# Attention on one core: V's gate logits carried beside V, tokens on partitions, and another split of PSUM

## The chip, the cores and the metric

One core of one Trainium2 chip. The time is device microseconds of one execution. The kernel before took 1797.77 us at the median of three runs (1797.65 to 1798.2).

## What is computed

An attention whose keys and values are averages over eight neighbours feeds a top-2 mixture of eight experts, and that feeds a dense block. Cut to what matters:

```python
# q, k, v: 8 batches, 8 heads, 576 tokens, head dimension 64
k_p, v_p = mean of k, v over groups of 8 tokens          # 72 per head
attn = softmax(q @ k_p.T / 8)                            # 576 x 72
x = (attn @ v_p), heads side by side                     # 4608 tokens x 512

logits = x @ w_gate                                      # 8 experts
noisy = logits + log1p(exp(x @ w_noise)) * noise
top 2 of noisy, softmax over the two
out = sum over the two experts of weight * (relu(x @ w1[e]) @ w2[e])

h = out @ w_in;  result = (h - tanh(h)) @ w_out
```

## The kernel before

The program runs three stages after each other: `attention` (L1113 on), `moe` and `Moe2`. The first takes some 252 of 1796 us. Its work is 36 tiles of 128 tokens (`NT`), and a hand-written loop of `NT + 6` steps at its end issues, in each step, one stage of several tiles: exponentials of tile t, the transposes of the weights of tile t - 2 (`st_attT`), q's transposes of tile t + 2 (`st_q`), the scores of tile t + 1, the gate projection of tile t - 5 (`st_x`), the scaling of tile t - 6 (`st_g`), and last the weights times V of tile t - 3 (`st_av`). Every engine takes its instructions in the order in which this loop issues them; tiles in PSUM are handed on as soon as their reader is through.

A batch has 576 tokens, four and a half tiles, so tiles 4, 13, 22 and 31 belong to two batches. The 576 keys of eight heads (72 each) lie on partitions in five chunks of 128, 128, 128, 96 and 96 (`cuts`), so a chunk holds parts of up to three heads. For each batch `prep_jobs` averages k and v by halving adds (on GpSimd first, then VectorE), finds V's largest magnitude (`vmaxT`), makes a power-of-two scale from it and builds `VB`, a block matrix of V in which columns of a head are zero on rows of other heads (`vscale`, masked by `of`), and builds `KB` for the scores (`kbd`). The steps of these jobs are fixed relative to the batch's first tile `T0`; `chain` and `fixed` place VectorE's other work (the weights of the first expert: `amax`, `low`) in the steps with the least planned load.

Weights times V (L1349 to L1359) holds V as the stationary operand and the transposed weights as the moving one, so the result has features on partitions; ScalarE copies it (`st_xT`, L1361), and `st_x` (L1365) multiplies it with `wgn`, an identity with the gate's and the noise's columns beside it, which turns tokens onto partitions and makes 16 logits a head pair at once. `st_g` (L1376) reads both from `px`, divides by the softmax sums, writes x to DRAM and collects the logits.

```python
nc.tensor.matmul(p[:, m, o:o + n], VB[b % 2][:w, c, j:j + 128], a[:w, c, o:o + n], ...)      # st_av
nc.tensor.matmul(p[:, m, 0:128 + 4 * E], xT[:, m], wgn[:, m], start=True, stop=True)         # st_x
tt(xr..., h(p[:, :, 0:128], D), r..., op=OP.mult)                                            # st_g, L1381
tt(lg[:, t - t0], h(p[:, :, 128:128 + 4 * E], 2 * E), r..., op=OP.mult)                      # st_g, L1387
```

PSUM has eight banks: `px` one buffer of two banks, `pt` four buffers (transposes, V products, all batch jobs and gates), `psc` two (one per half of a tile's scores).

Groups of tiles (up to 9, 19, 28 and 35) go through `gate_jobs`, a chain of some 45 small VectorE operations that `tick` spreads over the steps; `tick_pe` lets one TensorE part of it through per step. After the second group `early_x` gathers the first expert's first 512 tokens. The last steps (t from 36) have no scores any more and a few idle matmuls (`warm`).

In `moe`, units of L1 and L2 follow each other with a lag of two; after the first group's last unit (`u == KF - 1`) two L2 are issued, then the transposes `tr` of the second group's three blocks through PSUM (L333 to L336), then the next L1.

Of the kernel before, what the change touches and what calls it, by code (L numbers as in the profile page):

```python
# [186 lines left out]
def moe(nc, tc, st, V, z):  # L187
# [410 lines left out]
    for u in range(len(units) + LAG):  # L598
# [514 lines left out]
def attention(nc, tc, st, V):  # L1113
# [52 lines left out]
    def warm(n, tag="px"):  # L1166

        if tag == "px":
            p = ps.tile([128, HP, 256], F32, name="px", bufs=1)[:, 0:2].rearrange("p a c -> p (a c)")
        else:  # L1170
            p = ps.tile([128, 4 * SP], F32, name=tag, bufs=2)
        for _ in range(n):
            nc.tensor.matmul(p, calm[:, 0:128], calm[:, 0:p.shape[1]], start=True, stop=True)
# [11 lines left out]
    VB = [one.tile([128, 5, 4 * D], F32, name=f"vb{i}") for i in range(2)]  # L1185
# [27 lines left out]
    for i in range(2):  # L1213
        for w, o in ((w_gate, 0), (w_noise, E)):
            o += 128 + 2 * E * i
            nc.sync.dma_start(wgn[64 * i:64 * i + 64, :, o:o + E], w.rearrange("(m i p) e -> i p m e", i=2, p=64)[i])
# [11 lines left out]
    lz = ep.tile([128, NT, 2 * E], F32, name="lz")  # L1228
    def prep_jobs(b, first=False):
# [20 lines left out]
        def vmaxT():  # L1250
            p = ps.tile([1, 128], F32, name="pt", bufs=4)
            nc.tensor.transpose(p, tl["vm"], identf)
            yield
            tl["vx"] = wk.tile([1, 1], F32, name="vx")
            nc.vector.tensor_reduce(tl["vx"], p, axis=AX.X, op=OP.max)

        def vscale():
            p = ps.tile([128, 1], F32, name="pt", bufs=4)
# [4 lines left out]
            of8 = wk.tile([128, 5, 4], F32, name="of8")  # L1263
            ts(of8, of, m[:, 2:3], None, op0=OP.mult)
            (nc.gpsimd if b > 1 else nc.vector).tensor_tensor(VB[b % 2].rearrange("p c (j d) -> p c j d", d=D), tl["va"][:, :, 0:1].to_broadcast([128, 5, 4, D]),
               of8[:, :, :, None].to_broadcast([128, 5, 4, D]), op=OP.mult)
# [7 lines left out]
            ts(isc[:, f0:f1], m[:, 1:2].to_broadcast([128, f1 - f0]), 1.0 / 128, None, op0=OP.mult)  # L1274

        def kbd():
            for i, (c0, c1) in enumerate(((0, 3), (3, 5))):
                w = cuts[c1] - cuts[c1 - 1]
                p = ps.tile([128, 4, 128], F32, name="pt", bufs=4)[:, 0:c1 - c0, 0:w]
# [9 lines left out]
    def st_q(t):  # L1289
        p = ps.tile([128, HP, 128], F32, name="pt", bufs=4)  # L1290
# [20 lines left out]
    def st_exps(t):  # L1311
        at = wk.tile([128, 2, 4, SP], F32, name="at", bufs=3)
        if t in sums:
            SM[0] = wk.tile([128, 5, 2, 4], F32, name="sm"), t
# [5 lines left out]
        if t + 1 in sums or t + 1 == NT:  # L1320
            SM[1] = sm, t0

    def st_norm(t):
        if not (t + 1 in sums or t + 1 == NT):
            tick(2)
            return
        sm, t0 = SM.pop(1)
        sm = sm[:, 0:t + 1 - t0]
        ts(sm, sm, 1e-9, None, op0=OP.add)
        tick()  # L1330
        rc = wk.tile([128, 5, H], F32, name="rc")[:, 0:t + 1 - t0]
# [5 lines left out]
    def st_attT(t):  # L1337
# [3 lines left out]
        for g, (c0, c1) in enumerate(((0, 3), (3, 5))):  # L1341
            w = cuts[c1] - cuts[c1 - 1]
            p = ps.tile([128, 4, 128], F32, name="pt", bufs=4)[:w, 0:c1 - c0]
# [5 lines left out]
    def st_av(t):  # L1349
        a = ATT.pop(t)  # L1350
        p = ps.tile([128, HP, 128], F32, name="pt", bufs=4)
        for o, n, b, s in runs(t):
            for m in range(HP):
                cs = [c for c in range(5) if cuts[c] < 2 * SP * (m + 1) and 2 * SP * m < cuts[c + 1]]
                for c in cs:
                    w, j = cuts[c + 1] - cuts[c], 128 * (m + 1 - c)
                    nc.tensor.matmul(p[:, m, o:o + n], VB[b % 2][:w, c, j:j + 128], a[:w, c, o:o + n],
                                     start=(c == cs[0]), stop=(c == cs[-1]))
        PV[t] = p  # L1359

    def st_xT(t):  # L1361
        XT[t] = wk.tile([128, HP, 128], F32, name="xT")
        nc.scalar.activation(XT[t], PV.pop(t), AF.Copy)

    def st_x(t):  # L1365

        xT = XT.pop(t)
        p = PX[t] = ps.tile([128, HP, 256], F32, name="px", bufs=1)
        for m in range(HP):
            nc.tensor.matmul(p[:, m, 0:128 + 4 * E], xT[:, m], wgn[:, m], start=True, stop=True)  # L1370

    PX = {}
# [3 lines left out]
    def st_g(t):  # L1376
        p, rc = PX.pop(t), RC.pop(t)
        xr = wk.tile([128, DM], F32, name="xr", bufs=3)
        r = rc.rearrange("p (m i) -> p m i", i=2)[:, :, :, None]
        h = lambda a, n: a.rearrange("p m (i n) -> p m i n", n=n)  # L1380
        tt(xr.rearrange("p (m i n) -> p m i n", m=HP, i=2), h(p[:, :, 0:128], D), r.to_broadcast([128, HP, 2, D]), op=OP.mult)  # L1381
        nc.sync.dma_start(x_d[128 * t:128 * t + 128, :], xr)
        if t in sums:
            LG[0] = wk.tile([128, 5, HP, 2, 2 * E], F32, name="lg", bufs=2)
            LG[1] = t
        lg, t0 = LG
        tt(lg[:, t - t0], h(p[:, :, 128:128 + 4 * E], 2 * E), r.to_broadcast([128, HP, 2, 2 * E]), op=OP.mult)  # L1387
# [346 lines left out]
```

## Time and profile before

| | before |
|---|---|
| median of 3 runs | 1797.77 us |
| the profiled execution, its own time | 1798.16 us |
| its span, first to last instruction | 1795.9 us |
| TensorE busy | 1756.3 us (98%) |
| VectorE busy | 1284.9 us (72%) |
| ScalarE busy | 939.9 us (52%) |
| GpSimd busy | 269.8 us (15%) |
| mean granted TensorE clock | 0.995 |

The profile gives for each engine the time in which at least one of its instructions ran. PE is TensorE's matmuls, PEld its weight loads (they overlap matmuls), DVE VectorE, ACT ScalarE, POOL GpSimd, SP the engine that issues most transfers. Matmuls are pipelined: the time between the starts of two is less than the duration shown of one. A matmul of 32-bit numbers appears as two passes, each with its weight load; a transpose as one. An arrow behind an idle time names what ended it.

### The profile page before, as it was taken

The page shows a single profiled execution, that of the slowest core. Times are in us where ns is not written, and L with a number is a line of the kernel's source. Part 1 is how long each engine was busy: PE and PEld are TensorE (multiplying, and loading weights), DVE is VectorE, ACT ScalarE, POOL GpSimd, SP SyncE. Part 2 cuts the span into 40 slices and gives each one's busy share as a digit, 9 for nine tenths or more (in the row PEclk, how much of TensorE's full clock was granted, in tenths as well). Part 3 has the DMA queues.
Part 4 walks back from the last instruction along what each step waited for, and adds up shares of the span by engine and source line. Part 5 has one row for each costly group of instructions (what it writes and reads, how often), then busy time and mean ns, then how long its engine had stood idle before and what let it go on. Part 6 is the DMA issues. An engine that isn't in the chain of part 4 may idle for free. (4 is left out here: it accounts for less than half of the span.)

```text
span 1795.9 us, 28933 instructions
## 1 busy us (share of the span) xinstructions
PE 1756.3 (98%) x10792; PEld 1071.3 (60%) x10792; DVE 1284.9 (72%) x2550; ACT 939.9 (52%) x2249; POOL 269.8 (15%) x264
## 2 busy tenths in 40 slices
PE   7999989999999999999999999999999999999998
PEld 5998864545455454545454454566666666666664
DVE  5688776776767666665665457687887879788775
ACT  5887732434435343434334246575665756566554
POOL 2334101303031030101101102010120201010000
PEclk8999999999999999999999999999999999999999
DMA  9877214565664446555544435330322314041100
GB/s 222 230 183 210 78 65 142 129 161 147 189 170 130 141 127 188 135 141 142 143 129 102 119 85 137 96 94 19 95 70 46 94 34 95 19 95 47 37 25 25
DMA packets 264157, 203.44 MB, mean 113 GB/s; under 512 B 188160, under 2 KB 208640, under 8 KB 264000
## 3 DMA queue, kind: packets, MB, share of 16 engines
q1 hardware_dynamic: 251840, 162.16, 34.1%
q0 software_dynamic: 11904, 38.81, 8.6%
q8 instruction: 88, 1.44, 0.3%
q14 instruction: 69, 0.57, 0.1%
q10 hardware_dynamic: 256, 0.46, 0.1%
HBM read 121.82 MB, written 45.74 MB: 93 GB/s over the span
## 5 line engine op out<-in xcount | busy, mean ns | idle before, releaser
L359 ACT ACTIVATE hT<-ph 128x512 f16<-128x512 f32 (+2 forms) x192 | 96.8, 504 | 437.6 <-PE ph L357 437.5
L355 PE MATMUL ph<-xTp,pair 128*128 128x384 f16 (+2 forms) x736 | 245.5, 334 | 1.5 <-PEq L455 0.8
L356 PE MATMUL ph<-xTp,pair 128*128 128x384 f16 (+2 forms) x736 | 245.0, 333 | 0.4 <-DVE xTp L336 0.4
L357 PE MATMUL ph<-xTp,pair 128*128 128x384 f16 (+2 forms) x736 | 245.0, 333 | 0.0
L360 DVE SCALAR_TENSOR_TENSOR hT<-ph,hT 128x512 f16<-128x512 f32 (+2 forms) x192 | 110.8, 577 | 174.8 <-ACT hT L359 174.6
L1045 PE MATMUL py<-wo,gT 128*128 128x512 f16 x576 | 218.4, 379 | 1.0 <-DVE gT L992 1.0
L1043 PE MATMUL py<-wo,gT 128*128 128x512 f16 x576 | 218.4, 379 | 0.1
L377 PE MATMUL py<-pair,hT 128*128 128x512 f16 x576 | 218.4, 379 | 0.0
L378 PE MATMUL py<-pair,hT 128*128 128x512 f16 x576 | 218.4, 379 | 0.0
L379 PE MATMUL py<-pair,hT 128*128 128x512 f16 x576 | 218.4, 379 | 0.0
L1044 PE MATMUL py<-wo,gT 128*128 128x512 f16 x576 | 218.4, 379 | 0.0
L902 PEld LDWEIGHTS <-wi 128*128 128x128 f16 x1536 | 150.2, 98 | 58.6 <-issue 0.2
L315 POOL DMA_INDIRECT xg<-x_d,idx x75 | 77.6, 1035 | 666.9 <-DVE xp L342 508.8
L716 POOL DMA_INDIRECT y<-y_d,ridx x64 | 78.8, 1232 | 517.0 <-DVE y L727 240.7
L355 PEld LDWEIGHTS <-pair 128*128 128x128 f16 x768 | 75.0, 98 | 73.8 <-issue 14.2
L356 PEld LDWEIGHTS <-pair 128*128 128x128 f16 x768 | 75.1, 98 | 57.2 <-issue 0.9
L357 PEld LDWEIGHTS <-pair 128*128 128x128 f16 x768 | 75.1, 98 | 57.1 <-issue 0.6
L1002 ACT ACTIVATE th<-th,bias 128x512 f32<-128x512 f32 x144 | 102.5, 712 | 3.3 <-DVE th L1000 3.3
L1003 DVE SCALAR_TENSOR_TENSOR th<-th,t 128x512 f32<-128x512 f32 x144 | 98.6, 685 | 1.4 <-ACT th L1002 1.4
L992 DVE TENSOR_TENSOR gT<-th,gT 128x512 f16<-128x512 f32 x144 | 98.8, 686 | 0.2 <-ACT gT L991 0.2
L999 DVE SCALAR_TENSOR_TENSOR t<-hb,cinf,hs 128x512 f32<-128x512 f32 x64 | 48.0, 750 | 70.9 <-ACT hs L998 70.9
L1045 PEld LDWEIGHTS <-gT 128*128 128x128 f16 x576 | 56.3, 98 | 69.3 <-DVE gT L992 1.5
(306 smaller groups left out, 3506.8 us busy)
## 6 DMA issues: line engine op xcount, KB each, us to landing
stage<-in_moe_w SPq DMA_DIRECT2D x64, 512.0 KB, 6.3
y_d<-ys SPq DMA_DIRECT2D x82, 256.0 KB, 4.1
x_d<-xr SPq DMA_DIRECT2D x36, 256.0 KB, 2.3
out<-o SPq DMA_DIRECT2D x36, 256.0 KB, 2.3
qt<-in_q SPq DMA_DIRECT2D x32, 256.0 KB, 6.6
raw<-in_moe_w_in SPq DMA_DIRECT2D x32, 256.0 KB, 3.4
raw<-in_moe_w_out SPq DMA_DIRECT2D x32, 256.0 KB, 3.6
kt<-in_k SPq DMA_DIRECT2D x7, 768.0 KB, 5.5
```

Source lines behind the costliest of these rows:

```text
L355: nc.tensor.matmul(p[:, :nt], w[:, 0, m, s], x[:, 0, m, :nt], start=(m == 0), stop=False)
L356: nc.tensor.matmul(p[:, :nt], w[:, 0, m, s], x[:, 1, m, :nt], start=False, stop=False)
L357: nc.tensor.matmul(p[:, :nt], w[:, 1, m, s], x[:, 0, m, :nt], start=False, stop=(m == KD - 1))
L360: stt(h[:, 1, :nt], p[:, :nt], 0.0, h[:, 0, :nt], op0=OP.max, op1=OP.subtract)
L377: nc.tensor.matmul(p, h[:, 0, s], w[:, 0, f], start=(f == 0), stop=False)
L378: nc.tensor.matmul(p, h[:, 0, s], w[:, 1, f], start=False, stop=False)
L379: nc.tensor.matmul(p, h[:, 1, s], w[:, 0, f], start=False, stop=(f == KF - 1))
L902: nc.tensor.matmul(p, w[:, a, m], y[:, c, b, m], start=(start and m + x == 0), stop=(m == 1 and x == 2), skip_group_check=True)
L1002: nc.scalar.activation(q, q, AF.Square, bias=bias[:, 2:3], scale=SP5)
L1043: nc.tensor.matmul(p, g[:, 0, s], wo[:, 0, f], start=(f == 0), stop=False)
L1044: nc.tensor.matmul(p, g[:, 0, s], wo[:, 1, f], start=False, stop=False)
L1045: nc.tensor.matmul(p, g[:, 1, s], wo[:, 0, f], start=False, stop=(f == KF - 1))
```

## The change

`wgn`, `st_xT` and `st_x` go. Per batch, V itself is transposed (`vmaxT`), multiplied with the gate's and the noise's weights of its heads (`vscale`), and the 16 results stand beside the head's 64 columns in `VB`, now [128, 5, 3, 80]. `st_av` holds the transposed weights as the stationary operand and `VB` as the moving one, so tokens come out on partitions and it writes `px` itself, in two banks of four heads. On GpSimd the V part of `VB` is built in five pieces. The loop has `NT + 4` steps: `st_g` works on tile t - 4. `pt` has three buffers, `psc` three. The batch jobs' TensorE work comes behind the scores instead of at the step's start, all but the last job of a step complete; V's jobs come one step earlier, the first expert's maximum, `high` and `low` a step or two later. Softmax sums are grouped by four tiles. In `moe` the transposes of the second group's first block come ahead of the two L2, those of the others between them.

```diff
@@ moe
         if u == KF - 1:
+            tr(1, 0)
             L2(*units[u - 1])
+            for j in range(1, n):
+                tr(1, j)
             L2(*units[u])
-            for j in range(n):
-                tr(1, j)
@@ attention
-            p = ps.tile([128, HP, 256], F32, name="px", bufs=1)[:, 0:2].rearrange("p a c -> p (a c)")
+            p = ps.tile([128, 2, 512], F32, name="px", bufs=1)[:, 0]
...
-    VB = [one.tile([128, 5, 4 * D], F32, name=f"vb{i}") for i in range(2)]
+    VB = [one.tile([128, 5, 3, D + 2 * E], F32, name=f"vb{i}") for i in range(2)]
...
-    wgn = one.tile([128, HP, 128 + 4 * E], F32, name="wgn")
-    nc.vector.memset(wgn[:, :, 128:], 0.0)
-    nc.vector.tensor_copy(wgn[:, :, 0:128], identf[:, None, :].to_broadcast([128, HP, 128]))
+    wg = one.tile([64, H + 1, 2 * E], F32, name="wg")
+    nc.vector.memset(wg[:, H:], 0.0)
...
+    hb = (0, 1, 3, 5, 6)
...
         def vmaxT():
-            p = ps.tile([1, 128], F32, name="pt", bufs=4)
+            p = ps.tile([1, 128], F32, name="pt", bufs=3)
             nc.tensor.transpose(p, tl["vm"], identf)
+            q = [ps.tile([64, 4, 128], F32, name="pt", bufs=3) for _ in range(2)]
+            for c in range(5):
+                nc.tensor.transpose(q[c // 4][:, c % 4], tl["va"][:, c, 0], identf)
             yield
...
+            tl["vT"] = wk.tile([64, 5, 128], F32, name="vT", bufs=1)
+            nc.scalar.activation(tl["vT"][:, 0:4], q[0], AF.Copy)
+            nc.scalar.activation(tl["vT"][:, 4], q[1][:, 0], AF.Copy)
         def vscale():
...
+            vg = ps.tile([128, 5, 3, 2 * E], F32, name="pt", bufs=3)
+            for c in range(5):
+                nc.tensor.matmul(vg[:, c].rearrange("p j e -> p (j e)"), tl["vT"][:, c],
+                                 wg[:, hb[c]:hb[c] + 3].rearrange("p h e -> p (h e)"), start=True, stop=True)
             yield
...
-            (nc.gpsimd if b > 1 else nc.vector).tensor_tensor(VB[b % 2].rearrange("p c (j d) -> p c j d", d=D), tl["va"][:, :, 0:1].to_broadcast([128, 5, 4, D]),
-               of8[:, :, :, None].to_broadcast([128, 5, 4, D]), op=OP.mult)
+            tt(vb[:, :, :, D:], vg, bc(2 * E), op=OP.mult)
...
+            e, cs = (nc.gpsimd, each) if b > 1 else (nc.vector, [(0, 5)])
+            for c0, c1 in cs:
+                s = slice(c0, c1)
+                e.tensor_tensor(vb[:, s, :, 0:D], tl["va"][:, s, 0:1].to_broadcast([128, c1 - c0, 3, D]), bc(D)[:, s], op=OP.mult)
...
     def st_scores(t):
-            p = ps.tile([128, 4, SP], F32, name="psc", bufs=2)
+            p = ps.tile([128, 4, SP], F32, name="psc", bufs=3)
...
     def st_av(t):
-        p = ps.tile([128, HP, 128], F32, name="pt", bufs=4)
+        p = PX[t] = ps.tile([128, 2, 512], F32, name="px", bufs=1)
+        n1 = D + 2 * E
         for o, n, b, s in runs(t):
...
+            for g, parts in enumerate((((0, 0, 2), (1, 0, 3), (2, 0, 1)), ((2, 1, 2), (3, 0, 2), (4, 0, 2)))):
+                for i, (c, j, w) in enumerate(parts):
+                    r, h = cuts[c + 1] - cuts[c], hb[c] + j - 4 * g
+                    nc.tensor.matmul(p[o:o + n, g, n1 * h:n1 * (h + w)], a[:r, c, o:o + n],
+                                     vb[:r, c, j:j + w].rearrange("p j n -> p (j n)"),
+                                     start=(i == 0), stop=(i == 2), skip_group_check=True)
...
-        at_pe(T0 + 1, job["vt"])
-        at_pe(T0 + 2, job["vs"])
-        fixed(T0 + 2, 2000)
+        at_pe(T0, job["vt"])
+        at_pe(T0 + 1, job["vs"])
+        fixed(T0 + 1, 1800)
...
-    for f, t in ((c1.fin1, 14), (c1.fin2, 16), (c2.fin1, 31), (c2.fin2, 33)):
+    for f, t in ((c1.fin1, 15), (c1.fin2, 17), (c2.fin1, 33), (c2.fin2, 34)):
...
-    chain(*((1024, 17 + j, 18 + j, lambda j=j: c1.low(j)) for j in range(4)))
+    chain(*((1024, 18 + j, 19 + j, lambda j=j: c1.low(j)) for j in range(4)))
...
-    for t in range(NT + 6):
+    for t in range(NT + 4):
...
-        if 0 <= t - 4 < NT:
-            st_xT(t - 4)
-        pj = [f() for f in pe_step.get(t, [])]
-        for g in pj:
-            next(g)
-        tick_pe()
...
-        if 0 <= t - 6 < NT:
-            st_g(t - 6)
+        if 0 <= t - 4 < NT:
+            st_g(t - 4)
...
         if t + 1 < NT:
             st_scores(t + 1)
-        if 0 <= t - 5 < NT:
-            st_x(t - 5)
+        pj = [f() for f in pe_step.get(t, [])]
+        for g in pj[:-1]:
+            both(g)
+        for g in pj[-1:]:
+            next(g)
+        tick_pe()
```

## Rows read from the trace of the kernel before

**Rows 1.** By stretch: length; PE, PEld, DVE, ACT, POOL; clock, DMA share, GB/s.

```profile
20.00:45.00 25.00, 19.49 (x128) 15.91 (x129) 17.58 (x34) 16.28 (x85) 6.41 (x8) 0.80 1.02 212
45.00:90.00 45.00, 44.07 (x372) 42.25 (x371) 29.96 (x66) 36.75 (x169) 14.31 (x19) 1.00 0.82 230
90.00:135.00 45.00, 43.12 (x358) 41.03 (x357) 39.22 (x98) 38.60 (x164) 13.58 (x16) 1.00 0.71 182
...
48.65:226.10 177.45, 169.87 (x1438) 161.39 (x1437) 141.70 (x347) 140.74 (x622) 53.26 (x58) 1.00 0.63 171
226.10:252.00 25.90, 20.95 (x168) 18.68 (x165) 20.30 (x54) 9.71 (x17) 1.89 (x2) 0.93 0.23 77
...
300.50:1795.90 1495.40, 1483.59 (x8753) 842.93 (x8752) 1065.02 (x1982) 752.26 (x1468) 196.07 (x171) 1.00 0.40 104
```

**Rows 2.** TensorE timeline, steady attention: start us, us, what, count.

```profile
47.56 1.25 PE L1370 MATMUL px<-wgn,xT 128*128 128x160 f32 x8
48.65 1.95 PE L1357 MATMUL pt<-aT,vb 128*128 128x128 f32 x16
...
67.94 0.71 PE L1345 MATMUL pt<-identf,at 128*128 128x128 f32 x5
68.49 0.60 PE L1293 MATMUL pt<-identf,qt 128*128 128x128 f32 x4
68.93 1.15 PE L1303 MATMUL psc<-kb,qT 128*128 128x144 f32 x8
69.91 1.25 PE L1370 MATMUL px<-wgn,xT 128*128 128x160 f32 x8
...
109.27 3.68 PE L1357 MATMUL pt<-aT,vb 128*128 128x64 f32 x32
112.78 0.72 PE L1345 MATMUL pt<-identf,at 128*128 128x128 f32 x5
...
224.32 1.95 PE L1357 MATMUL pt<-aT,vb 128*128 128x128 f32 x16
226.11 0.66 PE L1173 MATMUL psc<-calm 128*128 128x288 bf16 x4
```

**Rows 3.** Waits in 48.65 to 226.10 us, TensorE and VectorE: total, times, longest.

```profile
PE px L1370 <- DVE lg L1387: 2.2, 2, 1.4
...
DVE mx L1306 <- PE psc L1303: 25.9, 14, 4.1
```

**Rows 4.** Groups in 48.65 to 226.10 us, shapes apart: busy, mean ns, idle before.

```profile
L1363 ACT ACTIVATE xT<-pt 128x512 f32<-128x512 f32 x30 | 18.1, 605 | 9.6 <-PE pt L1357 9.5
...
L1381 DVE TENSOR_TENSOR xr<-px,rc 128x512 f32<-128x512 f32 x31 | 20.8, 671 | 1.7 <-PE px L1370 1.7
L1387 DVE TENSOR_TENSOR lg<-px,rc 128x128 f32<-128x128 f32 x31 | 8.6, 278 | 0.0
...
L1265 POOL TENSOR_TENSOR vb<-vt,of 128x1280 f32<-128x1280 f32 x6 | 14.0, 2332 | 94.8 <-DVE of L1264 61.8 <-DVE isc L1274 33.0
```

**Rows 5.** VectorE's operation at line 1274: ns min/median/max, first and last start.

```profile
L1274 DVE TENSOR_SCALAR isc<-vs x8: 150/163/2329, 36.9 to 213.6; 128x4 f32<-128x4 f32 x8
```

**Rows 6.** TensorE timeline at the start.

```profile
23.55 0.37 PE L1252 MATMUL pt<-identf,vm 128*1 128x128 f32 x1 [4.13 <-DVE vm L1248]
```

**Rows 7.** TensorE timeline at the end of the attention.

```profile
244.61 2.47 PE L1370 MATMUL px<-wgn,xT 128*128 128x160 f32 x8 [2.47 <-DVE lg L1387]
```

**Rows 8.** TensorE timeline around the second group's transposes.

```profile
296.15 0.38 PE L378 MATMUL py<-pair,hT 128*128 128x512 f16 x1
296.36 0.38 PE L379 MATMUL py<-pair,hT 128*128 128x512 f16 x1
...
300.66 0.32 PE L356 MATMUL ph<-xTp,pair 128*128 128x384 f16 x1 [0.40 <-DVE xTp L336]
```

**Rows 9.** Loads of q: from issue to landing, all of the execution.

```profile
DMA to landing us min/median/max: 3.2/6.4/10.6
```

More of the change, by code (lines that the diff above doesn't have):

```diff
@@ L1168, in warm @@
         if tag == "px":
-            p = ps.tile([128, HP, 256], F32, name="px", bufs=1)[:, 0:2].rearrange("p a c -> p (a c)")
+            p = ps.tile([128, 2, 512], F32, name="px", bufs=1)[:, 0]
         else:
-            p = ps.tile([128, 4 * SP], F32, name=tag, bufs=2)
+            p = ps.tile([128, 4 * SP], F32, name=tag, bufs=3)
         for _ in range(n):
@@ L1212, in attention @@
     load_q(3)
[L1213 to L1216, printed above, removed]
+    for w, o in ((w_gate, 0), (w_noise, E)):
+        nc.sync.dma_start(wg[:, 0:H, o:o + E], w.rearrange("(h p) e -> p h e", p=64))
     load_kv(1, "v")
@@ L1228, in attention, with head_mask @@
     lz = ep.tile([128, NT, 2 * E], F32, name="lz")
+    hb = (0, 1, 3, 5, 6)
+    hm = one.tile([128, 5, 3], F32, name="hm")
+    lm = one.tile([128, 5, 3], F32, name="lm")
+    for c0, c1, base, step in ((0, 1, 0, 0), (1, 4, 56, -16), (4, 5, 48, 0)):
+        nc.gpsimd.iota(hm[:, c0:c1], pattern=[[step, c1 - c0], [-SP, 3]], base=base, channel_multiplier=1,
+                       allow_small_or_imprecise_dtypes=True)
+    def head_mask():
+        ts(lm, hm, float(SP), 8.0, op0=OP.is_lt, op1=OP.mult)
+        ts(hm, hm, 0.0, None, op0=OP.is_ge)
+        tt(hm, hm, lm, op=OP.mult)
     def prep_jobs(b, first=False):
@@ L1278, in kbd @@
                 w = cuts[c1] - cuts[c1 - 1]
-                p = ps.tile([128, 4, 128], F32, name="pt", bufs=4)[:, 0:c1 - c0, 0:w]
+                p = ps.tile([128, 4, 128], F32, name="pt", bufs=3)[:, 0:c1 - c0, 0:w]
                 for c in range(c0, c1):
@@ L1289, in st_q @@
     def st_q(t):
-        p = ps.tile([128, HP, 128], F32, name="pt", bufs=4)
+        p = ps.tile([128, HP, 128], F32, name="pt", bufs=3)
         qt = QL.pop(t)
@@ L1312, in st_exps @@
         at = wk.tile([128, 2, 4, SP], F32, name="at", bufs=3)
-        if t in sums:
-            SM[0] = wk.tile([128, 5, 2, 4], F32, name="sm"), t
+        if t % 4 == 0:
+            SM[0] = wk.tile([128, 4, 2, 4], F32, name="sm"), t
         sm, t0 = SM[0]
@@ L1319, in st_exps @@
                 nc.scalar.activation(at[:, g, j], p[:, j], AF.Exp, bias=mx[:, j:j + 1], accum_out=sm[:, t - t0, g, j:j + 1])
-        if t + 1 in sums or t + 1 == NT:
+        if t % 4 == 3:
             SM[1] = sm, t0
     def st_norm(t):
-        if not (t + 1 in sums or t + 1 == NT):
+        if t % 4 != 3:
             tick(2)
@@ L1327, in st_norm @@
         sm, t0 = SM.pop(1)
-        sm = sm[:, 0:t + 1 - t0]
         ts(sm, sm, 1e-9, None, op0=OP.add)
         tick()
-        rc = wk.tile([128, 5, H], F32, name="rc")[:, 0:t + 1 - t0]
+        rc = wk.tile([128, 4, H], F32, name="rc")
         nc.vector.reciprocal(rc, sm.rearrange("p t a b -> p t (a b)"))
@@ L1342, in st_attT @@
             w = cuts[c1] - cuts[c1 - 1]
-            p = ps.tile([128, 4, 128], F32, name="pt", bufs=4)[:w, 0:c1 - c0]
+            p = ps.tile([128, 4, 128], F32, name="pt", bufs=3)[:w, 0:c1 - c0]
             for c in range(c0, c1):
@@ L1350, in st_av @@
         a = ATT.pop(t)
-        p = ps.tile([128, HP, 128], F32, name="pt", bufs=4)
+        p = PX[t] = ps.tile([128, 2, 512], F32, name="px", bufs=1)
+        n1 = D + 2 * E
         for o, n, b, s in runs(t):
[L1353 to L1370, printed above, removed]
+            vb = VB[b % 2]
+            for g, parts in enumerate((((0, 0, 2), (1, 0, 3), (2, 0, 1)), ((2, 1, 2), (3, 0, 2), (4, 0, 2)))):
[4 more added lines that the diff above has]
+                                     start=(i == 0), stop=(i == 2), skip_group_check=True)
     PX = {}
@@ L1561, in first @@
             add(nc.gpsimd, b, nm, 4, slice(*c))
-    for t in range(15, 35):
+    for t in range(13, 35):
         fixed(t, 1300)
@@ L1608, in early_tr @@
     def early_tr(j, x):
-        p = ps.tile([128, HP, 128], F32, name="pt", bufs=4)
+        p = ps.tile([128, HP, 128], F32, name="pt", bufs=3)
         for m in range(HP):
@@ L1623, in attention @@
         at(5 + j, c1.load, [j])
-        at(16 + j, c1.high, j, nc.scalar)
+        at(17 + j, c1.high, j, nc.scalar)
         at(22 + j, c2.load, [j])
@@ L1663, in attention @@
         tick()
-        for f, g in zip(pe_step.get(t, []), pj):
-            if f.__name__ == "kbd":
-                next(g, None)
         if t + 1 < NT:
             st_scores(t + 1)
-        if 0 <= t - 5 < NT:
-            st_x(t - 5)
+        pj = [f() for f in pe_step.get(t, [])]
[4 more added lines that the diff above has]
+        tick_pe()
         tick()
-        for g in pj:
+        for g in pj[-1:]:
             next(g, None)
```

28 lines of the change are left out of this document (15 added, 13 removed).

## The prediction

> **What bounds the kernel now.** I read the page's busy times first, then the busy time of each engine by stretch, then the TensorE timeline, then the waits. TensorE leads the page's busy times. From 300.5 us to the end it is busy for 1483.59 of 1495.40 us [rows 1] with expert and dense matmuls that the change leaves alone, so whatever is won or lost before 300.5 us reaches the end one for one. The reader is to see that this is a question about the first sixth of the span.
>
> In the steady part of the attention (48.65 to 226.10 us) TensorE is busy for 169.87 of 177.45 us at a granted clock of 1.00, VectorE for 141.70 and ScalarE for 140.74 [rows 1]. One step of the loop is one tile of 128 tokens: from the weights-times-V of one tile (48.65) to that of the thirtieth after it (224.32) is 175.67 us [rows 2], so 5.86 us a step, with some 5.6 us of TensorE, 4.7 of VectorE and 4.6 of ScalarE in it. TensorE is the bound, VectorE is not far behind: it stood idle for 25.9 us, 14 times, waiting for the scores, while TensorE waited for VectorE at `px` only twice, 2.2 us [rows 3].
>
> **The change, part by part.** The sum is made against the profiled execution (1798.2 us, of which 1795.9 are the span; the median of the runs shown is 0.4 us below it).
>
> *Attention times V.* Before, a tile costs 16 passes of 128 columns in 1.79 us (224.32 to 226.11) and then 8 passes of 160 columns through `wgn` in 1.09 us (47.56 to 48.65): 2.88 us [rows 2]. Passes of 144 columns take 0.98/8 = 0.122 us, of 160 take 0.136, so 0.84 ns a column; a pass of 64 columns still takes 3.51/32 = 0.110 us (109.27 to 112.78) [rows 2], which is the floor that a weight load sets. After, weights and tokens change places: six matmuls, two passes each, of 160, 240, 80 and 160, 160, 160 columns. Four at 0.136, one at 0.203 (0.136 plus 80 columns) and one at the floor of 0.11: 0.86 us, twice: 1.72 us. An unsplit tile saves 1.16 us; a tile that two batches share went from 3.51 + 1.09 to 24 such passes, 3.43, and saves 1.17. The 240-column pass is not in the trace: between 0.136 (nothing for more columns) and two floors, 0.22; I take 0.203 from the slope. Over the 31 tiles of the steady stretch, four of them shared: 36.0 us.
>
> *V's logits, new.* Per batch five transposes (five of the weights take 0.55 us, 67.94 to 68.49 [rows 2]) and ten passes of 48 columns at the floor, 1.1: 1.65 us. Seven batches in the stretch: 11.6 us back. Net 24.4 us of TensorE, 0.80 a step. On ScalarE the copy `xT` goes (0.605 us a tile [rows 4]); two copies of V come, each at most that row's 0.605, a batch every 4.5 tiles: from 4.6 to 4.3 us a step, nothing on the path while TensorE needs more. On VectorE comes one product of 240 PSUM columns a batch, between the rows of 128 (0.278) and 512 columns (0.671) [rows 4], 0.39 by columns, under 0.1 a step. The two reads of `px` keep their size; their new stride I cost at nothing, with VectorE's slack as the cover, and bound by the row's own size, 0 to 0.1 us a step.
>
> *GpSimd's V blocks.* One product of 1280 elements at 2.33 us, six times, becomes five of 192: by elements 1.75 us, at GpSimd's price in more pieces perhaps 3. GpSimd is busy for 53.26 of 177.45 us [rows 1], and the first user is two steps later. While the old product runs, a VectorE operation of four elements takes up to 2.329 us instead of 0.163 [rows 5]; the pieces come after it now. So VectorE gets back between 0 and 6 x 2.2 = 13 us; I take 4, since the median of that row is undisturbed and only some of the eight meet it. The Trainium skill (SBUF — State Buffer, "Who interferes with whom") says that the second to issue blocks until the first one's instruction ends; the trace agrees with the 2.329 us. By that rule five pieces could each block something, and VectorE would get back about 13 - 10.5 (six times 1.75) = 2.5 us, an estimate, and the forecast would be 1768.5.
>
> *What the stretch comes to.* TensorE alone would give 177.45 - 24.4 = 153.1 us. VectorE then has about 141.70 + 2.7 - 4 = 140 us to do in it, 92%, in uneven steps (a step carries a weight reduction, a gate chain or neither). `px` has one buffer. Before, its reading by `st_g` had 1.79 us of another tile's matmuls more before TensorE wrote it again; now only transposes, `st_q` and scores stand between, 0.55 + 0.44 + 0.98 = 2 us [rows 2], of which the two reads take 0.95 [rows 4]. So where VectorE is a microsecond late TensorE waits, and nothing but that microsecond covers it. I take VectorE at 88 to 90% of the new stretch, a little over its share in its densest part before (39.22 of 45.00 us [rows 1], 87%): 158 us, 19 saved. The ends are 5 and 29 (24 and 5 of the 7.6 us that TensorE stood idle).
>
> *Three halves of scores, three general buffers.* TensorE waits in the stretch for scores' buffers do not appear; the third half only matters at the start. Three general buffers for three allocations a step (four for four before): none to 0.2 us a step of waits for ScalarE's copies, within the ends above.
>
> *Start.* Batch jobs behind the scores: at 23.55 TensorE had stood 4.13 us before V's maximum with q's transposes and the scores behind it [rows 6]. These (some 3 us at that clock) now fill the wait. The moved jobs' loads are the same; the queue of loads is full until 45 us (DMA share 1.02 [rows 1]), which holds back what the first V product can gain. I take 3.5, between 0 and 7. The jobs moved by a step later (`fin1`, `high`, `low`) end nearer to the second weight's load, behind which q's loads wait on SP; those land in 6.4 us at the median, 10.6 at most [rows 9], against two steps' lead: 11.7 us now, 10.5 then. Cost: nothing, at worst a few waits.
>
> *End of the attention.* The pipe is two steps shorter: 36 + 4 instead of 36 + 6. The last stretch takes 25.90 us, VectorE busy for 20.30 of it [rows 1] and TensorE waiting up to 2.47 us for it [rows 7]. Two pairs of `st_g` (1.9 us) leave it and the third gate group starts two steps earlier, so some 16 of its operations, about 4 us, leave it too; these then lie in the four steps before, where they take back some of it. I take 6, between 3 and 9.
>
> *Transposes between.* From the end of the last L2 matmul (296.36 and a pitch of 0.21) to where matmuls run on (300.66) are 4.1 us with 12 transposes in them, 12 x 0.11 = 1.3 us [rows 8]. One L2 (12 x 0.21 = 2.5 us) between the first block and the others and one behind them cover the copies: 2.6 of the 2.8 us saved, between 1 and 2.8. The rows they read were gathered long before.
>
> Sum: 19 + 3.5 + 6 + 2.6 = 31.1. 1798.2 - 31.1 = **1767 us**.
>
> **Rivals.** *VectorE is the bound at once*, uneven steps cost more: 8 in the stretch, 2 at the start, 4.5 at the end, 2.6: 1781. For it: 87% before. Against: its 25.9 us of idle before the scores.
> *TensorE's whole saving arrives*: 29 + 6 + 7 + 2.6: 1753. For it: ScalarE and GpSimd get lighter; against: the single `px`.
> *No change*: the loads (0.82 of the DMA's time from 45 to 90 us at the old pace [rows 1]) and VectorE between them hold every step where it was, and what start and end give goes into TensorE's new waits for `px`: 1797.
> *Slower, by the single `px`*: place, the V product at each step's end, waiting for `st_g` of the tile before. Price w in each of 31 steps; the other terms give 12 and the stretch 0.80 a step, so it decides from w = 1.2 us. With the whole 1.79 us of lost lead as w: 1798 + 55 - 24 - 12 = 1817. For it: the 2.47 us wait at that place [rows 7]. Against: two such waits in the steady part [rows 3].
> *Slower, by the clock*: with a larger share of transposes TensorE's clock falls from 2.4 to 1.2 GHz for part of the stretch. Its 146 us of work at the lower level for half of it: 146 x 1.5 = 219, 42 longer, less 12: 1828; it decides from 30%. Rows: 1.00 in the stretch with a step's 9 transposes in it, 0.80 at the start [rows 1]. The Trainium skill (TensorE: Matmul & The Clock Gate, "Part 4: PE-mode transpose") says that transposes don't count as activity for the clock; by that rule the share matters, and the row of 1.00 speaks against that it is enough.
>
> **How the numbers follow.** Forecast 0.60, VectorE at once 0.17, whole saving 0.10, no change 0.05, slower by `px` 0.06, by the clock 0.02. A run tells about 0.2% (3.6 us) from no change. Faster 0.87, same 0.05, slower 0.08. The range goes from the whole saving with a start of 7 and an end of 9 (1750) to the low ends, 5 + 0 + 4 + 2 (1787).
>
> **What would show it.** Right: V products of about 1.7 us a tile, a step of about 5.2 us, expert matmuls from about 224 us, no stop at the transposes of the second group. The `px` step is wrong if TensorE's waits for `lg` at the V product pass 0.3 us a step; the VectorE step if VectorE is under 85% with TensorE not waiting; the clock if the stretch shows under 1.00. The forecast is wrong if the steady step stays above 5.6 us.

## The result, and the profile after

The changed kernel takes 1775.24 us at the median of five runs (1773.64 to 1779.65), the kernel before 1797.77 us beside it: a ratio of 0.9886, with a 95% interval of 0.9873 to 0.9898, or 22.5 us less. The prediction said 1767 us, between 1750 and 1787. The profiled execution after has a span of 1773.4 us, 22.4 us shorter than the 1795.9 of before; the parts below are made against these two spans.

Busy time by stretch, cut at the same pieces of work in both kernels: the third to the thirty-third V product (30 steps); from there to the first expert matmul; to the first matmul of the second group; to the end. Columns as in [rows 1]. Before:

```profile
48.65:224.32 175.67, 168.09 (x1422) 159.61 (x1421) 140.21 (x342) 140.74 (x622) 53.26 (x58) 1.00 0.64 172
224.32:252.03 27.71, 22.73 (x184) 20.46 (x182) 21.83 (x59) 9.71 (x17) 1.89 (x2) 0.94 0.22 73
252.03:299.93 47.90, 44.65 (x226) 21.18 (x227) 29.65 (x103) 10.66 (x19) 4.94 (x5) 1.00 0.32 105
```

After:

```profile
44.03:205.47 161.44, 145.74 (x1141) 135.02 (x1140) 139.94 (x358) 125.22 (x604) 58.41 (x85) 0.97 0.71 195
205.47:225.84 20.37, 15.98 (x102) 13.69 (x102) 14.83 (x40) 6.80 (x15) 0.00 (x0) 0.83 0.22 78
225.84:274.75 48.91, 45.02 (x235) 21.80 (x235) 33.52 (x110) 11.71 (x20) 4.94 (x5) 1.00 0.35 108
274.75:1773.40 1498.65, 1484.12 (x8755) 843.25 (x8753) 1063.73 (x1981) 752.37 (x1468) 196.34 (x171) 1.00 0.40 103
```

| part | saved | forecast |
|---|---|---|
| start, to the third V product (48.65 to 44.03) | 4.6 | 3.5 |
| 30 steady steps (5.86 to 5.38 us each) | 14.2 | 19 |
| end of the attention (27.71 to 20.37) | 7.3 | 6 |
| first expert matmul to the second group (47.90 to 48.91) | -1.0 | 2.6 |
| the rest (1495.97 to 1498.65) | -2.7 | 0 |
| sum | 22.4 | 31.1 |

What the reader is to see in the first line of each fence: TensorE's work in the 30 steps fell by 22.35 us, but its idle time rose from 7.58 to 15.70 us, and the granted clock fell from 1.00 to 0.97. VectorE kept its 140 us and is now busy for 87% of the stretch instead of 80%.

The new V product in TensorE's timeline (columns as in [rows 2]). From one start to the next instruction it is 49.54 - 47.82 = 1.72 us unsplit, 2.93 for a tile that two batches share; ten passes of V's logits take 1.24:

```profile
47.82 1.88 PE L1381 MATMUL px<-vb,aT 128*128 128x160 f32 x12
49.54 0.71 PE L1368 MATMUL pt<-identf,at 128*128 128x128 f32 x5
...
52.09 2.99 PE L1381 MATMUL px<-vb,aT 128*64 128x160 f32 x24
55.02 0.76 PE L1368 MATMUL pt<-identf,at 128*128 128x128 f32 x5
...
65.66 1.31 PE L1278 MATMUL pt<-wg,vT 64*128 64x48 f32 x10
```

The waits of the 30 steps (total us, times, longest), which answer to [rows 3]. VectorE's idle time before the scores went from 25.9 to 3.0 us; in its place TensorE waits for VectorE before the V product:

```profile
PE px L1381 <- DVE lg L1400: 6.4, 4, 3.6
PE pt L1501 <- DVE l_row L1496: 2.7, 3, 1.3
PE pt L1275 <- ACT aT L1369: 2.4, 2, 1.6
...
DVE mx L1330 <- PE psc L1327: 3.0, 7, 0.7
```

The longest of these waits, from VectorE's side. A maximum of the second weight's chunk (`am`) and three gate operations stand ahead of the two reads of `px`; TensorE had been ready for 3.56 us when `lg` ended:

```profile
147.55 1.21 DVE L127 TENSOR_REDUCE am<-stage 128x1 f32<-128x1024 f32 x1
148.68 1.67 DVE L1436 SCALAR_TENSOR_TENSOR g_p<-g_p,g_th 128x80 f32<-128x80 f32 x3
150.27 0.68 DVE L1394 TENSOR_TENSOR xr<-px,rc 128x512 f32<-128x512 f32 x1
150.88 0.27 DVE L1400 TENSOR_TENSOR lg<-px,rc 128x128 f32<-128x128 f32 x1
```

And TensorE's V products around low clock, each after a wait; the undisturbed ones take 1.88 to 1.98 us (2.99 for a shared tile). The first line is a wait of 1.79 us with no low clock behind it (1.00 from 97.27 to 105.00 us):

```profile
97.27 2.99 PE L1381 MATMUL px<-vb,aT 128*64 128x160 f32 x24 [1.79 <-DVE lg L1400]
...
114.03 0.38 PE L1275 MATMUL pt<-vx,onec 1*128 1x1 f32 x2 [1.65 <-ACT aT L1369]
116.40 3.46 PE L1381 MATMUL px<-vb,aT 128*128 128x160 f32 x12
...
151.20 5.65 PE L1381 MATMUL px<-vb,aT 128*64 128x160 f32 x24 [3.56 <-DVE lg L1400]
...
219.24 3.70 PE L1381 MATMUL px<-vb,aT 128*128 128x160 f32 x12 [3.04 <-DVE lg L1400]
```

At the second group's transposes, which answer to [rows 8], the copies are covered (the L1 matmul at 274.75 follows without a gap), but the third block's tokens come late. Their gather, on GpSimd, is issued at 264.80, 6.9 us ahead of the transposes; before, the last gather was issued at 279.99, 16.6 us ahead of the first transposes at 296.58. Three lines of TensorE's timeline after, and the gather's from GpSimd's; then the two of before:

```profile
268.88 0.60 PE L333 MATMUL pt<-identf,xg 128*128 128x128 f32 x4
271.69 0.63 PE L333 MATMUL pt<-identf,xp 128*128 128x128 f32 x4 [2.21 <-DMA xp<-x_d,idx]
...
274.75 0.33 PE L355 MATMUL ph<-xTp,pair 128*128 128x384 f16 x1
...
264.80 1.16 POOL L315 DMA_INDIRECT xp<-x_d,idx  x1 [0.30 <-issue]
```

```profile
279.99 1.16 POOL L315 DMA_INDIRECT xp<-x_d,idx  x1 [0.30 <-issue]
...
296.58 1.04 PE L333 MATMUL pt<-identf,xg 128*128 128x128 f32 x8
```

### The profile page after: what moved, and what is told of

It reads as the page before. It is cut to its first block, busy times and chain, and to the rows that moved or that the text cites. A ratio compares the mean times of both kernels' runs of the same rounds, so it can differ in the third digit from the quotient of the medians.

```text
span 1773.4 us, 28294 instructions
## 1 busy us (share of the span) xinstructions
PE 1727.0 (97%) x10456; PEld 1040.7 (59%) x10456; DVE 1282.9 (72%) x2562; ACT 922.4 (52%) x2229; POOL 276.3 (16%) x291
## 5 line engine op out<-in xcount | busy, mean ns | idle before, releaser
L355 PEld LDWEIGHTS <-pair 128*128 128x128 f16 x768 | 75.0, 98 | 76.2 <-issue 16.6
```

The lines of the kernel that those rows point to most:

```text
L355: nc.tensor.matmul(p[:, :nt], w[:, 0, m, s], x[:, 0, m, :nt], start=(m == 0), stop=False)
```

## The experiments

Theory: TensorE's work fell as costed, and VectorE's lateness at single steps (with the low clock behind the longest waits) ate what is missing in the steps; at the handover to the experts the gate's chain, pushed behind the first expert matmul, made the gathers late. Rivals: the scarcer PSUM buffers, one pair by one, hold TensorE; or the moved parts themselves (batch jobs, transposes) cost what they were to save. A third stands beside every trace: the clock can fall in one execution and not in another of the same code (see `a_gate`). Every ratio is to the kernel before, with its 95% interval.

**The transposes alone, in the kernel before** (`b_tr`).

```diff
+            tr(1, 0)
             L2(*units[u - 1])
+            for j in range(1, n):
+                tr(1, j)
             L2(*units[u])
-            for j in range(n):
-                tr(1, j)
```

> The kernel before with only the expert stage's transposes moved between the two L2. Theory (the changed kernel lost its gain at these transposes because its gate chain, and with it the gather, ends late): in the kernel before the gather was issued 14 us ahead of the earlier place, so nothing waits there and the 2.6 us of the forecast appear: about 1795 us, 0.9986 of before. Rival (the moved transposes cost as much as they give, by breaking the run of matmuls): within 0.5 us of before.

1794.97 us, 0.9983 (0.9975 to 0.9992). No transposes wait, and the stage from the first expert matmul to the second group goes from 47.90 to 45.86 us: the term of 2.6 us holds (2.0) where the rows are there in time.

```profile
292.74 0.60 PE L333 MATMUL pt<-identf,xg 128*128 128x128 f32 x4
293.18 0.60 PE L333 MATMUL pt<-identf,xp 128*128 128x128 f32 x4
...
296.20 0.33 PE L355 MATMUL ph<-xTp,pair 128*128 128x384 f16 x1
```

**The change with the transposes back behind both L2** (`a_notr`), the same diff the other way round.

> The changed kernel with the transposes back behind both L2. Late gate: the wait of 2.2 us for the third gather goes, the 2.8 us of uncovered copies come back: 1775 to 1777 us. Rival (the moved transposes are the loss themselves): 1771 to 1773.

1777.38 us, 0.9891 (0.9873 to 0.991), against 0.9886 for the change: no difference that these runs can tell. Its stage takes 48.57 us instead of 48.91. In the changed kernel the move brings nothing, since what the copies no longer cost is spent waiting for the gather.

**The gate's chain let through after the first units too** (`a_gate`).

```diff
-gate(6, u > 1)
+gate(6, True)
```

> The changed kernel, in which the expert stage lets a TensorE part of the gate through in its first two units already. Late gate: the third group's remaining list goes through two units earlier (the fourth group's chain starts behind it), the gather is issued some 6 to 10 us earlier and the 2.2 us wait at the transposes goes: 1772 to 1774. Rival (TensorE then stops for the list's rows in the first unit and loses as much): 1775 to 1777.

1777.01 us, 0.9887 (0.987 to 0.9905). The wait is gone (the blocks' transposes at 264.16, 267.18 and 267.62 follow without one), but the time is not better, much as the expectation's rival had it. From the first expert matmul to the second group it takes 49.24 us, where the change takes 48.91 with the wait: TensorE now stops for 2.90 us ahead of the fourth group's first gate matmuls, instead of 1.14, and the clock is at 0.91 from 221.41 to 240.00 us, low behind that stop.

```profile
235.40 0.19 PE L1457 MATMUL pt<-mb,before 128*128 128x64 bf16 x1 [2.90 <-DVE mb L1453]
```

The rest of the execution takes 1504.55 instead of 1498.65, with single waits of 2.3 and 2.5 us there (until 475.91 and 963.82) that the change does not have, and a clock of 0.5 behind each. Why these waits come is not settled. The late gather is shown as the cause of the wait, not as a loss that is had back by this edit.

This run tells one thing more. Its edit, and that of `a_notr`, lie behind the first expert matmul in program order, so up to there all three executions ran the changed kernel's code. They differ all the same: from the first to the last V product it takes 185.43 us in the change, 185.57 in `a_notr` and 184.11 in `a_gate`, and from the last V product to the first expert matmul 6.60, 6.57 and 4.16. In `a_gate` the same waits of 1.65 and 3.04 us have no low clock behind them:

```profile
113.89 0.38 PE L1275 MATMUL pt<-vx,onec 1*128 1x1 f32 x2 [1.65 <-ACT aT L1369]
...
217.25 1.96 PE L1381 MATMUL px<-vb,aT 128*128 128x160 f32 x12 [3.04 <-DVE lg L1400]
```

So a single profile can't credit an edit with one or two microseconds in the loop, or with the 2.4 us behind it.

**Two buffers for the scores** (`a_psc2`).

```diff
-ps.tile([128, 4, SP], F32, name="psc", bufs=3)
+ps.tile([128, 4, SP], F32, name="psc", bufs=2)
```

> The changed kernel with two halves of scores instead of three, nothing else. Forecast's view (the third half matters only at the start): 1775 to 1777. Rival (with shorter steps the scores wait for ScalarE's exponentials in each step): 8 us or more slower, 1783 and above.

1771.01 us, 0.985 (0.9834 to 0.9865): faster than the change, against the expectation. From the first to the last V product it takes 186.06 us against 185.43, less than two executions of one code differ by, so the third half shows no worth in the loop. In the profile the gain lies elsewhere: 2.4 us from the last V product to the first expert matmul, because the same wait there is followed by a V product at full clock (as in `a_gate`, which has three buffers), and 3.1 us in the rest, whose code is the same. Before the second group 1.5 us are lost again (50.44 against 48.91, at a clock of 0.97). The five runs go from 1767.71 us at a mean granted clock of 0.998 to 1775.46 at 0.990. So a gain by the buffers themselves is not shown.

```profile
219.10 1.96 PE L1381 MATMUL px<-vb,aT 128*128 128x160 f32 x12 [3.04 <-DVE lg L1400]
```

**`px` with three banks, of which a tile takes two** (`a_px3`), with two score buffers.

```diff
+    PXA = ps.tile([128, 3, 512], F32, name="px", bufs=1)
-        p = PX[t] = ps.tile([128, 2, 512], F32, name="px", bufs=1)
+        p = PX[t] = (PXA[:, 0:2], PXA[:, 0:3:2], PXA[:, 1:3])[t % 3]
```

> As the run with two halves of scores, and the free bank goes to px: three banks, so that one half of a tile's V product never waits for the reading of the tile before. Theory (the single px couples TensorE to VectorE's late steps): of 11.4 us of waits at px and 5.9 us of matmuls at the lower clock behind waits, half or more goes: 5 to 12 us faster than the run with two halves. Rival (VectorE's sum of work sets the pace, whatever the buffers): within 2 us of that run.

1773.13 us, 0.9856 (0.984 to 0.9872), and TensorE's waits at `px` are 10.5 us, 7 times, as with one buffer (11.1, 7 times). It tells nothing of the buffers, though: in the trace no half runs early; all passes of a tile, those into the free bank too, stand behind the longest wait. Presumably the program puts one wait on the three banks as a whole; that is not shown.

```profile
153.39 4.61 PE L1384 MATMUL px<-vb,aT 128*64 128x160 f32 x24 [3.40 <-DVE lg L1403]
```

**`px` doubled, with its control** (`a_px4`, `a_px1c`). Two whole buffers need two more banks: two for the scores, two general ones. V's maximum then shares a bank with two of V's transposes, the scale one with V's logits. The control has the same but one `px`.

```diff
-ps.tile([128, HP, 128], F32, name="pt", bufs=3)
+ps.tile([128, HP, 128], F32, name="pt", bufs=2)
...
-ps.tile([128, 2, 512], F32, name="px", bufs=1)
+ps.tile([128, 2, 512], F32, name="px", bufs=2)
```

> The change with two buffers for the scores' halves and two general buffers (V's maximum shares a bank with two of V's transposes, the scale one with V's logits), px as in the change: two banks in one buffer. It is the control for the run with px doubled, and prices the third general buffer. The prediction took 'none to 0.2 us a step' for three instead of four; if the step is set by VectorE, two buffers cost no more than that again: at most 6 us over the run with two score halves (1771.0), so 1771 to 1777, with TensorE's waits at pt for ScalarE's copies under 0.2 us a step. If the general buffers are what couples the engines, these waits pass 1 us a step and it is over 1790.

> The same with px in two buffers of two banks each, so that the V product of a tile never waits for the reading of the tile before. Theory: VectorE's work per step sets the pace, and TensorE's wait at px is only the place where its lateness shows; then the 11 us of waits at px go, but TensorE waits as long elsewhere (for the scores' maxima, or at pt), the stretch from the third to the thirty-third V product stays within 2 us of the control's, and the time within 3 us of it. Rival: the single px couples the two engines, and a late step is lost because nothing can be done ahead; then the waits at px (11.4 us in the change) and the low clock behind them (some 5.9 us) go and do not come back: 8 to 16 us below the control, and the stretch at 150 to 154 us against 161.4 in the change.

Control: 1800.0 us, 1.0018 (1.0008 to 1.0028), a clear miss (1771 to 1777 was expected); doubled: 1799.02 us, 1.0016 (1.0005 to 1.0028). The third general buffer, together with the shared banks that come with two, is worth 29 us (1800.0 to the 1771.0 of two score buffers alone); 15 of them lie in the 30 steps (177.48 to 162.33). With two, q's transposes wait in nearly every step for ScalarE's copy of the weights; in the control

```profile
PE pt L1318 <- ACT aT L1370: 26.2, 29, 3.1
PE px L1382 <- DVE lg L1401: 2.9, 2, 2.1
```

and with `px` doubled

```profile
PE pt L1318 <- ACT aT L1370: 28.0, 29, 3.1
```

The 2.9 us at `px` went and the general buffers took 1.8 us more. In this setting `px` is not what couples the engines, but the setting has another bound, so whether a second `px` would help the change itself stays open: with three general buffers and two for the scores there is no room for it in eight banks.

**The weight's maxima from a quarter of the columns**, in the change (`a_amax`) and in the kernel before (`b_amax`). These kernels take the first expert's scale from 256 of 1024 columns, which takes 7.2 us off VectorE and nothing else.

```diff
-self.stage[:, c], axis
+self.stage[:, c, 0:256 if self.e == 0 else 1024], axis
```

> The changed kernel; the eight reductions of the first expert's weights read a quarter of the columns (the scale is then taken from a quarter of the weights), 0.9 us less for VectorE in each of eight steps, 7.2 us in all. Theory (VectorE's late steps are what TensorE waits for): 4 to 8 us faster than the changed kernel. Rival (TensorE alone sets the pace, the waits are of other origin): within 1 us.

> The kernel before with the same shortened reductions (the scale is then taken from a quarter of the weights). Both theories: TensorE is the bound there, so at most 1.5 us faster than before; if it gains as much as the changed kernel does, VectorE's work was no covered work before either, and the forecast's reading of the bound was wrong.

Changed kernel: 1771.97 us, 0.9863 (0.9847 to 0.9879), 3.3 us below the change at the medians, less than the 4 to 8 expected, and the two intervals overlap. From the first to the last V product it takes 182.29 us, 1.8 to 3.3 less than the three executions of the change's attention code. Kernel before: 1797.65 us, 1.0001 (0.9992 to 1.001). The same 7.2 us of VectorE are worth nothing before and 2 to 3 us after: VectorE has become part of the bound, at single steps, and not the whole of it.

**Idle matmuls where TensorE waits** (`a_fill`), which add work and are to keep the clock up.

```diff
+        if t == 19:
+            warm(10, "psc")
...
+        if t in (25, 38):
+            warm(26, "psc")
         if 0 <= t - 3 < NT:
             st_av(t - 3)
```

> The changed kernel with idle matmuls (0.12 us each) put where its profile shows TensorE waiting and then at the lower clock: 10 behind the scores of step 19, 26 ahead of the V product of steps 25 and 38. Theory (the clock falls behind these waits, and costs 1.5 + 2.7 + 1.7 us): the fillers lie in the waits, the clock stays: 3 to 6 us faster. Rival (the clock falls for something else): the fillers cost what they last beyond the waits, 0 to 4 us slower.

1771.4 us, 0.9855 (0.9838 to 0.9871). The clock is at 1.00 in the three stretches, where the change has 0.66, 0.76 and 0.84:

```profile
115.00:120.00 5.00, 5.00 (x43) 4.48 (x42) 3.77 (x16) 5.00 (x21) 2.17 (x5) 1.00 0.69 236
145.00:155.00 10.00, 9.63 (x79) 8.14 (x78) 9.17 (x21) 6.25 (x35) 6.22 (x9) 1.00 0.76 220
205.00:226.00 21.00, 18.56 (x140) 15.03 (x141) 16.85 (x45) 8.31 (x21) 0.00 (x0) 1.00 0.24 85
```

From V product to V product over the first place it takes 14.24 us instead of 15.79, over the second 13.54 instead of 15.89, and from the last V product to the first expert matmul 4.16 instead of 6.60: 6.3 us together. Some 2 us of it are missing at the start: the V product of the first shared tile after 90 us begins at 99.34 instead of 97.27. 1.1 us of that are there at the third V product already, and 1.0 comes with the clock, which fell here ahead of all the idle matmuls and did not in the change (1.00 there):

```profile
85.00:95.00 10.00, 9.25 (x59) 8.77 (x58) 8.49 (x27) 6.60 (x35) 7.00 (x12) 0.83 0.87 237
```

Not all of the 6.3 us is the idle matmuls' doing: `a_gate`, which has none, took 14.65, 14.74 and 4.16 us at the same places. What speaks for them is the mean granted clock of whole executions: 0.996 to 0.998 in all four runs here, 0.990 to 0.995 in the 16 runs of the three kernels with the change's attention code. So the low clock behind the waits costs the change some 5 to 6 us in its profiled execution (against the same places in `a_gate` and here), and keeping it up gave 3.8 us at the medians.

**The batch jobs behind the scores, in the kernel before** (`b_batch`).

```diff
-        for g in pj:
-            next(g)
-        tick_pe()
...
         if t + 1 < NT:
             st_scores(t + 1)
+        pj = [f() for f in pe_step.get(t, [])]
+        for g in pj[:-1]:
+            both(g)
+        for g in pj[-1:]:
+            next(g)
+        tick_pe()
```

> The kernel before with only the batch jobs' TensorE work moved behind the scores (the second batch's keys one step earlier, all but the last job of a step complete at once). Theory: it is this part that fills the 4.13 us wait for V's maximum at the start; the first V product comes at 34 to 36 us instead of 38.86, the steady step stays 5.86 us, and the time falls by 3 to 5 us: about 1794. Rival: the start is set by the queue of loads, and the gain at the start came from the shorter pipe and the lighter steps; then the first V product stays within 1 us of 38.86 and the time within 1.5 us of the kernel before.

1794.83 us, 0.9987 (0.9978 to 0.9997). The wait for V's maximum shrinks from 4.13 us [rows 6] to 1.22, and the first V product comes at 32.97 instead of 38.86, earlier than expected:

```profile
23.25 0.27 PE L1252 MATMUL pt<-identf,vm 128*1 128x128 f32 x1 [1.22 <-DVE vm L1248]
...
32.97 2.05 PE L1357 MATMUL pt<-aT,vb 128*128 128x128 f32 x16
```

Of these 5.9 us, 5.5 are still there at the first expert matmul and 5.2 at the second group, but at the end only 2 to 3 (1.9 at the medians, below the 3 to 5 expected): the rest of the execution took 2.0 us longer with the same code. This part alone gives all that the change gains at the start (5.1 us at the first V product).

**The parts put together** (`a_best`): two score buffers, the idle matmuls, and the second weight's maxima two steps later.

```diff
-(1024, 24 + j, 27 + j, lambda j=j: c2.amax(j))
+(1024, 26 + j, 29 + j, lambda j=j: c2.amax(j))
```

> The change with two buffers for the scores' halves, the idle matmuls at steps 19, 25 and 38, and the second weight's maxima two steps later (26 to 32 instead of 24 to 30), so that none is ahead of the scaling of x at the 3.56 us wait of step 25. Theory: VectorE's late steps cost TensorE the wait and the low clock behind it; the fillers alone gave 1771.4, two score halves alone 1771.0 of which nothing lay in the steps, and the later maxima take up to 2.4 us of VectorE out of the steps where TensorE waits. If the gains add, 1765 to 1769, below both kernels and below each part. Rival: the fillers and two score halves mend the same low clock (that of the drain), and the maxima only move the late steps; then it stays within 2 us of 1771.

1785.54 us, 0.9931 (0.9918 to 0.9945): missed, 14 us behind either part alone. The idle matmuls write into a score buffer. With three there is a free one; with two they wait for ScalarE's exponentials of the scores that lie in it, and the clock falls there (0.82 from 120 to 145 us, 0.83 from 155 to 175):

```profile
119.32 2.56 PE L1174 MATMUL psc<-calm 128*128 128x288 bf16 x10 [3.45 <-ACT at L1343]
...
161.54 5.75 PE L1174 MATMUL psc<-calm 128*128 128x288 bf16 x26 [4.85 <-ACT at L1343]
```

So two parts that each ran some 4 us below the change were not to be had together in this form; what the later maxima did here was not taken apart. Each of the two alone beats both kernels (1771.0 and 1771.4 us); nothing that was run is faster.

## Why the prediction was right, and where it was off

**TensorE's work: right.** 1.72 us a tile was forecast and measured; the shared tile took 2.93 instead of 3.43 (its passes of 64 tokens were costed as full ones); the logits' ten passes 1.24 instead of 1.1. Busy time in the 30 steps fell by 22.35 us even with some of it at the lower clock; 24.4 was the forecast for 31 tiles.

**VectorE's work: right.** 139.94 us in the 30 steps; the forecast took 140 for a stretch of 31 tiles. Its product of 240 columns takes 0.407 us (forecast 0.39), and the `px` reads with their new stride 0.684 and 0.279 (0.671 and 0.278 [rows 4]):

```profile
L1394 DVE TENSOR_TENSOR xr<-px,rc 128x512 f32<-128x512 f32 x30 | 20.5, 684 | 9.2 <-PE px L1381 8.9
...
L1298 POOL TENSOR_TENSOR vb<-vt,of 128x192 f32<-128x192 f32 x30 | 15.0, 531 | 67.9 <-DVE of L1284 51.6 <-PE pt L1368 16.3
...
L1400 DVE TENSOR_TENSOR lg<-px,rc 128x128 f32<-128x128 f32 x30 | 8.4, 279 | 0.0
...
L1286 DVE TENSOR_TENSOR vb<-pt,of 128x240 f32<-128x240 f32 x7 | 2.9, 407 | 0.9 <-PE pt L1278 0.3
```

GpSimd's five pieces take 2.37 to 2.44 us from the first start to the last end (3.06 once), between the 1.75 and the 3 of the forecast. The operation of four elements that had taken up to 2.329 us (three of the eight took 2.30 or more) takes 0.472 at most, no longer than one piece (0.531). Over the eight VectorE got back 5.1 us, where the forecast took 4. The Trainium skill (SBUF — State Buffer, "Who interferes with whom") has the two engines' shared ports as an exclusive lock; the trace agrees, with the length of the piece in place of the length of the product.

**The steady stretch: the mis-sized term.** "I take VectorE at 88 to 90% of the new stretch" became 87%, and 19 us became 14.2. The place was named ("where VectorE is a microsecond late TensorE waits"), the size was not: waits of 6.4 us at `px`, some 6 for the gate's list (`l_row`) and for general buffers, and behind the longest of them the lower clock. The criterion of 0.3 us a step was not passed (6.4/30 = 0.21), the one on the clock was: 0.97, which was to be 1.00. The step came to 5.38 us, not to "about 5.2". The rival *slower by the clock* had the fall, not its cause or its size. Steps with nine transposes ran at 1.00 from 33 to 100 us after as they did before; the clock fell behind waits of 1.65 to 3.56 us, though not behind each of them. The Trainium skill (TensorE: Matmul & The Clock Gate, "Part 4: PE-mode transpose") says that a transpose does not count as busy in the same way; no run here parts that from the waits. The rival *VectorE is the bound at once* took 8 us for the stretch; the truth lies between it and the forecast, and `a_amax` shows VectorE's share in it: 7.2 us less work, 1.8 to 3.3 us less time in the loop.

**Three halves, three general buffers: right, by luck in the second.** The third half "only matters at the start": without it the loop took 0.6 us more, within what executions of one code differ by. Three general buffers cost 2.4 + 0.7 us in 30 steps, inside "none to 0.2 us a step". That TensorE waits 0.9 us a step with two (26.2 us, 29 times; the step itself 0.5 us longer) shows how near the edge lies, which the prediction did not see.

**Start and end of the attention: right.** 4.6 for 3.5, from the batch jobs as argued (`b_batch`); 7.3 for 6, with 2.4 kept back by the lower clock in this execution (6.60 us behind the last V product, 4.16 in `a_gate`). The low end of the forecast's range takes 4 and 2 us for the end and the transposes, where these terms themselves went down to 3 and 1; with those it is 1789 us, which changes nothing here.

**Transposes between: the step that failed.** "The rows they read were gathered long before" was read from the kernel before. The gathers wait for the end of the fourth group's gate chain; that chain's end is 25.5 us behind the first expert matmul before (277.49) and 36.5 after (262.30). The prediction counted "some 16 of its operations" of the third group's chain as leaving the end of the attention, and did not ask which of them come back behind the first expert matmul. Before, the last eight of the 18 matmuls of that group's list stood ahead of it (252.03); after, they stand 10.4 us behind it (225.84), and the fourth group's first gate matmuls 22.6 us behind it instead of 11.9. Before, then after:

```profile
250.20 0.73 PE L1488 MATMUL pt<-l_col,l_row 128*128 128x160 f16 x8 [0.56 <-DVE l_row L1483]
...
263.90 0.19 PE L1444 MATMUL pt<-mb,before 128*128 128x64 bf16 x1 [1.33 <-DVE mb L1440]
```

```profile
236.21 0.72 PE L1501 MATMUL pt<-l_col,l_row 128*128 128x160 f16 x8
...
248.43 0.19 PE L1457 MATMUL pt<-mb,before 128*128 128x64 bf16 x1 [1.14 <-DVE mb L1453]
```

Against the 45.86 us of `b_tr`, where the rows are there in time, the stage is 3.05 us longer; the wait of 2.21 us and the 0.56 us that the eight matmuls hold TensorE make up 2.8 of them.

**The rest, 2.7 us, is not explained.** The code from the second group on is the same, yet this stretch took 1495.5 to 1500.0 us in the profiles of thirteen of these fourteen kernels (1495.97 before, 1498.65 after), and 1504.55 in `a_gate`, by waits of one or two us in different places, in `a_gate` with the low clock behind them. One profile each can't tell a change from chance there.

## What to carry to other kernels

When the busiest engine's work is cut to a little above the second's, the gain is not the difference of the sums: look at which instructions of the second engine stand, in program order, ahead of the one that frees the shared buffer, step by step, and cost the longest of these queues, with the lower clock behind it as a risk and not as a fixed price. Work that is moved out of a last stretch comes back in the next one; follow its last consumer (here a gather) before a later cover is booked. And a buffer that looks spare may be what an idle filler or a copy lives on: price the edge (three to two) before a bank is given away. Before a microsecond of one trace is credited to an edit, look at what two executions of the same code differ by at that place.

## What was not expected of the hardware

The same wait left the clock low in one kernel and not in another: 3.04 us before the last V product were followed by 3.70 us of it in the change and by 1.96 us with two score buffers, with the same five groups of instructions ahead of both. In `a_gate`, whose code up to there is the change's own, they were followed by 1.96 us too. And a wait of 1.65 us at 114.03 was followed by a granted clock of 0.66 from 115 to 120 us; with two score buffers the idle time came there in three pieces of 0.21, 0.44 and 0.47 us, and the clock in that stretch was 0.66 too; in `a_gate` the same 1.65 us were followed by 1.00:

```profile
115.00:120.00 5.00, 5.00 (x46) 4.92 (x46) 3.92 (x15) 4.27 (x20) 3.54 (x7) 1.00 1.04 284
```

So neither the length of one wait nor the code tells whether the clock falls.
